# Packed attention and MoE: the narrowing of the first two weight steps placed later in the first attention

## The chip, the cores and the metric

The kernel runs on one core of a Trainium2 chip. Its time is the device time of one execution in microseconds (us). The median of the runs shown is 772.96 us (771.65 to 775.1, 3 runs). One more execution was recorded by the hardware profiler; every row quoted here is from such a record.

Engines go by their names in the profile: PE is the tensor engine's matmuls, PEld its weight loads, DVE the vector engine, ACT the scalar engine, POOL GpSimd, SP the engine whose queue issues the DMAs. Times within the record count from the span's start. L148 is line 148 of the kernel.

## What is computed

```python
q, k, v: (8, 8, 576, 64) float32   # batch, head, token, head dimension; q, k and p drawn 8 times larger
p: (8, 8, 32, 64) float32          # 32 packing vectors for each head
w_in: (512, 2048), w_out: (2048, 512)

def sm_attn(qq, kk, vv):
    s = scale * np.matmul(qq, kk.transpose(0, 1, 3, 2))
    s = s - np.max(s, axis=-1, keepdims=True)
    a = np.exp(s)
    a = a / (np.sum(a, axis=-1, keepdims=True) + 1e-09)
    return np.matmul(a, vv)

p_packed = sm_attn(p, k, v)                # 32 rows for each head
out = sm_attn(q, p_packed, p_packed)
x = out.transpose(0, 2, 1, 3).reshape(8 * 576, 512)
h = x @ w_in
g = h * np.clip(h + 3.0, 0.0, 6.0) / 6.0
return (g @ w_out).astype(np.float32)
```

The two weights reach the kernel as 64-bit floats, so it has to make 32-bit floats of them itself. This is what the text calls narrowing.

## The kernel before, in words

**Tiling.** The eight batches are taken one after another, 576 tokens each. The hidden dimension of 2048 is cut into 16 steps `f` of 128. The product of attention and `w_in` is never made from the attention's output: since the second attention multiplies its weights A (576 x 32 for each head) with the packed rows, the kernel makes M = packed rows x `w_in` once for each batch and then A x M. All large products are made in float32r with each operand split into an upper half (`hi`, a cast) and a lower half (`lo`, what the cast leaves), so a product is three matmuls: hi x hi, hi x lo, lo x hi.

**A weight's way.** `load_w(f)` (L114) loads 128 x 512 64-bit values of `w_in` or `w_out`. `narrowed` (L130) is a generator, advanced one piece at a time by `step(part, n)` and to its end by `rest(part)`:

1. ACT scales the low words (L142), then the high words (L144)
2. DVE shifts the high words (L148), then puts the sign back (L150)
3. POOL adds the low part (L154); the float32 value is done and the load's buffer is free

`w_out_step` (L160) goes on: ACT casts the upper half (`wo_hi`, L164) and DVE makes the lower half (`wo_lo`, L166). For `w_in` the next user is `u_m0` (L192), which makes M of one step: matmuls on PE (L198), a cast on ACT (`m_hi`, L209), the lower half on DVE (`m_lo`, L211). The buffers for the 64-bit values are two for each of `w_in` and `w_out`; steps 2 and 3 use other space (`early`), which batch 0's v and q hold before.

**The first attention** (`first_attention`, L461) makes batch 0's attention, which nothing can hide, and its order is written out by hand for PE, DVE, ACT and POOL, by the sequence of the calls at L706 to L804. Heads come in two groups of four: `b0` and `b1` are `s2(0)` and `s2(1)` (L632), the second scores and their softmax for one group. One `s2` makes, piece by piece: the scores (L641), two maxima (L665), the subtraction (L668) and exponential (L669), the sums (L672), their reciprocals (L674, L676), the normalisation on POOL for group 0 and on DVE for group 1 (L682, L685), two transpositions on PE (L694) with a cast each (`a_hi`, L700), and the lower halves (`a_lo`, L703). Group 1's scores need its packed rows: `pack(1)` makes them (L621, L629), `pt1` turns them (L347) and copies them into place (L351). `tq` and `turned_rest` turn q on PE (L542, L555) and copy it on ACT (L546, L562). `tail()` hands out four banks of PSUM in turn. `warm(n)` (L724) is `n` matmuls on zeros, used by nobody; how many stand where is the tuple `WARM` (L35). `gemm1(h, 0, g)` (L446) is the first product of step 0 for one group.

**The first MoE** (`first_moe`, L899) takes batch 0 through the 16 steps. In each step: the first product (`gemm1`, L453), M of the next step, the narrowing of `w_in` two steps ahead (`in_(f + 2)`), relu on ACT (L956) and the gate on DVE (L957), then the rest of `w_out` of the next step (`rest(out_(f + 1))`) and the first five pieces of `w_out` two steps ahead, the two halves of the gated value (`gh`, L965, on ACT; `gl`, L967, on POOL), and the second product of the step before (`gemm2`, L858). For steps 0 to 3 the order is again written by hand for the four engines, by the sequence of the calls; from step 4 (`IN_ORDER`) on a planner sets it, and batch 1's attention is woven in. SP's order is the planner's throughout. `first_moe` receives the weight generators as `first_attention` leaves them and goes on from where they stand. Batches 1 to 7 follow in `moe`.

Of the kernel before, what the change touches and what calls it, by code (L numbers as in the profile page):

```python
# [31 lines left out]
POOL = range(8, 13)  # L32


WARM = (3, 2, 2, 1, 3)  # L35


@with_exitstack
def packed_attention_moe(
# [90 lines left out]
    def narrowed(f, name):  # L130

        raw = raws.pop((name, f))
        if not wide_in:
            state["w", name, f] = raw
            return
        words = raw.rearrange("p (n two) -> p n two", two=2)  # L140
        low, high = words[:, :, 0], words[:, :, 1]
        nc.scalar.activation(out=low, in_=low.bitcast(U32), func=AF.Copy, scale=2.0 ** -29)  # L142
        yield
        nc.scalar.mul(high.bitcast(F32), high.bitcast(F32), 2.0 ** -112)  # L144
        yield
        x = w_in_at(f) if name == "in" else wp.tile([P, DM], F32, name="x_out")
        xi = x.bitcast(I32)
        nc.vector.tensor_scalar(out=xi, in0=high, scalar1=3, scalar2=None, op0=ALU.logical_shift_left)  # L148
        yield
        nc.vector.scalar_tensor_tensor(  # L150
            out=xi, in0=high, scalar=SIGN, in1=xi, op0=ALU.bitwise_and, op1=ALU.bitwise_or
        )
        yield
        nc.gpsimd.tensor_tensor(out=xi, in0=xi, in1=low, op=ALU.add)  # L154
        state["w", name, f] = x

    def w_in_step(f):
        yield from narrowed(f, "in")

    def w_out_step(f):  # L160
        yield from narrowed(f, "out")
        yield
        x = state.pop(("w", "out", f))
        nc.scalar.copy(out=wo_hi[:, f], in_=x)  # L164
        yield
        (nc.gpsimd if f in POOL else nc.vector).tensor_sub(out=wo_lo[:, f], in0=x, in1=wo_hi[:, f].bitcast(F32))  # L166
# [3 lines left out]
    def step(part, n=1):  # L170
        for _ in range(n):
            next(part, None)

    def rest(*parts):
        for part in parts:
            for _ in part:
                pass
# [268 lines left out]
    def gemm1(h, f, g):  # L446

        mh, ml = state["m", 0, 0]
        fs = slice((f % FPC) * P, (f % FPC + 1) * P)
        ah, al = state["a", 0, g]  # L450
        for hf in range(2):
            for i, (mm, aa) in enumerate(((mh, ah), (mh, al), (ml, ah))):
                nc.tensor.matmul(  # L453
                    h[:, hf, :HS],
                    mm[:, g, fs],
                    aa[:, hf * HS:(hf + 1) * HS],
                    start=(g == 0 and i == 0),
                    stop=(g == NG - 1 and i == 2),
                )

    def first_attention():  # L461


        def tail():
            return ps_o.tile([P, 512], F32, name="ps_t", tag="acc")
# [83 lines left out]
        def turned_rest(nats, copy):  # L549

            t = gp.tile([P, 2, REM], F32, name="qtr0", tag="osb", bufs=2)
            ps = tail()[:, :2 * REM]
            for x, nat in enumerate(nats):
                for h in range(2):
                    nc.tensor.matmul(  # L555
                        ps[64 * h:64 * h + 64, x * REM:(x + 1) * REM],
                        nat[:REM, h, 4],
                        ident[:REM, :REM],
                        start=True,
                        stop=True,  # L560
                    )
            copy(out=t.rearrange("p x r -> p (x r)"), in_=ps)  # L562
            return t
# [160 lines left out]
        def warm(n):  # L724
            ps = tail()
            for _ in range(n):
                nc.tensor.matmul(ps[:, :2 * P], zeros[:, :P], zeros, start=True, stop=True)

        warm(WARM[0])
        act, dve = nc.scalar.copy, nc.vector.tensor_copy  # L730
# [20 lines left out]
        win0, wout0 = w_in_step(0), w_out_step(0)  # L751
# [8 lines left out]
        b0, b1 = s2(0), s2(1)  # L760
        m0, m1 = u_m0(0, tail), u_m0(1, tail)
        win1, wout1 = w_in_step(1), w_out_step(1)
        step(b0)
        rest(win0)
        step(wout0, 3)
        step(win1, 2)
        step(b0, 3)
        pack(1, *et1, r1, v1)
        step(tq[2])
# [1 line left out]
        qt.append(next(tq[2]))  # L771
        step(tq[3])
        qtr.append(turned_rest((q2, q3), act))
        rest(win1)
        rest(pt1)
        qt.append(next(tq[3]))
        step(b0, 4)
        step(wout0, 2)
        step(wout1, 2)
        step(b1)  # L780
        step(b0, 2)
        step(m0, 2)
        step(b1, 3)
        rest(m0)
        rest(b0)
        step(m1, 2)
        step(wout0)
        win2, wout2 = w_in_step(2), w_out_step(2)
        step(win2, 2)
        step(wout2, 2)  # L790
        warm(WARM[1])
        h = ps_h0.tile([P, 2, 512], F32, name="ps_h0", tag="w")
        gemm1(h, 0, 0)
        step(b1, 4)
        warm(WARM[2])
        step(b1, 2)
        warm(WARM[3])
        rest(m1)
        rest(b1)
        rest(wout0)  # L800
        step(wout1, 3)
        gemm1(h, 0, 1)
        warm(WARM[4])
        return h, {2: win2}, {1: wout1, 2: wout2}  # L804

    HAND = {mybir.EngineType.PE, mybir.EngineType.DVE, mybir.EngineType.Activation, mybir.EngineType.Pool}
# [236 lines left out]
```

## Time and profile before

| what | value |
| --- | --- |
| median of the runs shown | 772.96 us |
| the profiled execution: its time | 772.0 us |
| the profiled execution: its span, first to last instruction | 770.2 us |
| mean granted clock of PE | 0.991 |
| PE / DVE / ACT / POOL busy over the span | 741.4 / 374.2 / 388.6 / 288.5 us |
| PE busy in 0 to 40 us, by tens | 7.86, 9.44, 7.71, 8.36 |
| DVE busy in 0 to 40 us, by tens | 1.60, 6.36, 6.23, 8.85 |
| DVE busy in 40 to 100 us, by tens | 8.83, 9.90, 10.00, 9.93, 9.93, 9.81 |

The page gives the engines' busy time over the whole span and in 40 slices, then the chain that ended last. For one stretch, the windows view gives each engine's busy time in it, and the timeline gives the instructions with start, duration, engine, line, operation, output and inputs, and in brackets how long the engine had stood idle and what ended that. "x8" joins eight instructions of one kind. An instruction's duration can hold time in which it waits for a port, and the last 0.07 us or so of one overlap the next on its engine.

### The profile page before, as it was taken

The numbers are of one execution on the slowest core, as the hardware profiler recorded it, in microseconds if no ns is written. First come the engines' busy times: TensorE is split into PE (matmuls) and PEld (weight loads), VectorE is DVE, ScalarE is ACT, GpSimd is POOL, SyncE is SP. The second block draws the span as 40 slices with busy tenths as digits, with TensorE's granted clock in tenths as the row PEclk, the third lists the DMA queues.
The fourth block names the chain that finished last, engine by engine and source line by source line (L and its number), as shares of the span: only waits on it lengthen the run. The fifth ranks groups of instructions, "written<-read, shape, count | busy, mean of one in ns | idle before, by whom it ended". The sixth has DMA issues, their size and how long they took to land.

```text
span 770.2 us, 14036 instructions
## 1 busy us (share of the span) xinstructions
PE 741.4 (96%) x5197; PEld 585.9 (76%) x5197; DVE 374.2 (49%) x741; ACT 388.6 (50%) x922; POOL 288.5 (37%) x420
## 2 busy tenths in 40 slices
PE   8888778999999999999999999999999999999998
PEld 6666566778877786788787886878777887888886
DVE  3799989824283428342553528333452427321111
ACT  4667775455254535563354635454354545453343
POOL 0376795432223323433333332343333233343332
PEclk9999799999999999999999999999999999999999
DMA  8848993213340424015220344005330210000010
GB/s 248 253 108 191 220 244 71 46 55 62 67 103 1 89 66 90 1 46 102 49 65 1 74 82 90 1 29 93 65 73 1 59 33 28 1 29 0 1 42 29
DMA packets 191205, 55.98 MB, mean 73 GB/s; under 512 B 173216, under 2 KB 184480, under 8 KB 191136
## 3 DMA queue, kind: packets, MB, share of 16 engines
q1 hardware_dynamic: 191136, 55.08, 31.1%
q8 instruction: 41, 0.67, 0.4%
q14 instruction: 28, 0.23, 0.1%
HBM read 45.61 MB, written 9.44 MB: 71 GB/s over the span
## 4 chain that ended last, share of the span: by engine, by line
PE 77%; DVE 10%; DMA 5%; issue 3%; SPq 2%; ACT 2%; POOL 1%; DVEq 0%; POOLq 0%; ACTq 0%
PE acc L858 45%; PE ps_hh L829 22%; PE ps L270 6%; DMA raw_in<-in_moe_w_in_dram 2%; DVE tr L403 2%; PE ps L325 1%; DMA nat<-in_k_dram 1%; DVE wo_lo L166 1%; SPq L218 1%; DVE x_out L148 1%; DVE w_in_sb L150 1%; DMA raw_out<-in_moe_w_out_dram 1%; PE ps_h L453 1%; DMA v_nat<-in_v_dram 1%; PE ps L309 1%
## 5 line engine op out<-in xcount | busy, mean ns | idle before, releaser
L847 POOL TENSOR_TENSOR g<-t,g 128x256 fp32r<-128x256 f32 x224 | 167.5, 751 | 411.2 <-ACT g L846 385.1
L858 PE MATMUL acc<-wo_hi,g 128*128 128x512 f32 x896 | 316.7, 395 | 1.5 <-ACT g L846 1.5
L842 DVE SCALAR_TENSOR_TENSOR t<-t,ps_hh 128x320 f32<-128x320 f32 (+1 forms) x224 | 100.1, 449 | 251.8 <-ACT t L841 251.8
L841 ACT ACTIVATE t<-ps_hh,three 128x320 f32<-128x320 f32 (+1 forms) x224 | 112.5, 503 | 178.2 <-PE ps_hh L829 169.9
L858 PEld LDWEIGHTS acc<-wo_hi,g 128*128 128x128 f32 x896 | 167.9, 188 | 36.0 <-issue 4.0
L858 PE MATMUL acc<-wo_lo,g 128*128 128x512 f32 x448 | 177.5, 396 | 0.0
L846 ACT CAST g<-t 128x256 fp32r<-128x256 f32 x224 | 90.3, 405 | 93.1 <-DVE t L842 91.9
L829 PE MATMUL ps_hh<-a_hi,m_hi 128*128 128x320 f32 (+1 forms) x448 | 136.3, 305 | 0.3 <-DVE t L842 0.2
L829 PE MATMUL ps_hh<-a_lo,m_hi 128*128 128x320 f32 (+1 forms) x448 | 132.8, 296 | 0.0
L829 PE MATMUL ps_hh<-a_hi,m_lo 128*128 128x320 f32 (+1 forms) x448 | 132.7, 296 | 0.0
L829 PEld LDWEIGHTS ps_hh<-a_hi,m_hi 128*128 128x128 f32 x448 | 84.4, 189 | 34.5 <-issue 19.9
L858 PEld LDWEIGHTS acc<-wo_lo,g 128*128 128x128 f32 x448 | 84.5, 189 | 11.9 <-issue 1.7
L829 PEld LDWEIGHTS ps_hh<-a_lo,m_hi 128*128 128x128 f32 x448 | 84.5, 189 | 8.1 <-issue 0.9
L829 PEld LDWEIGHTS ps_hh<-a_hi,m_lo 128*128 128x128 f32 x448 | 84.5, 189 | 1.7 <-issue 1.3
L403 DVE STREAM_TRANSPOSE tr<-nat 128x576 f32<-128x576 f32 x56 | 41.7, 764 | 27.7 <-DMA nat<-in_q_dram 11.1
L393 DVE TENSOR_TENSOR m_lo<-ps,m_hi 128x512 fp32r<-128x512 f32 x56 | 36.1, 683 | 35.1 <-ACT m_hi L392 35.1
L853 POOL TENSOR_TENSOR bnd_lo<-t,bnd_hi 128x64 fp32r<-128x64 f32 x112 | 38.6, 344 | 0.0
L392 ACT CAST m_hi<-ps 128x512 fp32r<-128x512 f32 x56 | 30.1, 589 | 10.1 <-PE ps_hh L829 8.2
L270 PE MATMUL ps<-w_in_sb,pps 64*32 64x512 f32 x448 | 34.3, 601 | 0.4 <-DVE m_lo L393 0.4
L453 PE MATMUL ps_h<-a_hi,m_hi 128*128 128x288 f32 x64 | 20.9, 327 | 10.4 <-DVE t L957 9.5
L967 POOL TENSOR_TENSOR gl<-t,gh 128x512 fp32r<-128x512 f32 x16 | 23.1, 1446 | 19.4 <-ACT bnd_hi L966 14.7
L154 POOL TENSOR_TENSOR w_in_sb<-w_in_sb,raw_in 128x512 int32<-128x512 int32 x14 | 19.5, 1395 | 28.5 <-DVE w_in_sb L150 24.5
(175 smaller groups left out, 918.8 us busy)
## 6 DMA issues: line engine op xcount, KB each, us to landing
out_dram<-osb SPq DMA_DIRECT2D x36, 256.0 KB, 2.1
nat<-in_k_dram SPq DMA_DIRECT2D x112, 72.0 KB, 2.6
nat<-in_q_dram SPq DMA_DIRECT2D x112, 72.0 KB, 2.5
raw_in<-in_moe_w_in_dram SPq DMA_DIRECT2D x14, 512.0 KB, 5.0
raw_out<-in_moe_w_out_dram SPq DMA_DIRECT2D x14, 512.0 KB, 4.9
v_nat<-in_v_dram SPq DMA_DIRECT2D x56, 128.0 KB, 3.0
spare<-in_k_dram SPq DMA_DIRECT2D x2, 512.0 KB, 4.9
raw<-in_moe_w_in_dram SPq DMA_DIRECT2D x2, 512.0 KB, 3.9
```

The costliest lines, as they stand in the source:

```text
L270: nc.tensor.matmul(banks[x][NPK * a:NPK * a + NPK, :n], rows[half, a], c, start=True, stop=True)
L392: nc.scalar.copy(out=hi[:, x], in_=ps)
L393: nc.vector.tensor_sub(out=lo[:, x], in0=ps, in1=hi[:, x].bitcast(F32))
L403: nc.vector.transpose(out=t, in_=state.pop(("nat", which, b, a)))
L453: nc.tensor.matmul(h[:, hf, :HS], mm[:, g, fs], aa[:, hf * HS:(hf + 1) * HS], start=(g == 0 and i == 0), stop=(g == NG - 1 and i == 2),)
L829: nc.tensor.matmul(h[:, :n], mm[:, g, fs], aa[:, t0:t0 + n], start=(g == 0 and i == 0), stop=(g == NG - 1 and i == 2),)
L841: nc.scalar.activation(out=t[:, :n], in_=h, func=AF.Relu, bias=three)
L842: nc.vector.scalar_tensor_tensor(out=t[:, :n], in0=t[:, :n], scalar=6.0, in1=h, op0=ALU.min, op1=ALU.mult)
L846: nc.scalar.copy(out=gh, in_=tm)
L847: nc.gpsimd.tensor_sub(out=gl, in0=tm, in1=gh.bitcast(F32))
L853: nc.gpsimd.tensor_sub(out=bnd_lo[:, slot:slot + REM], in0=tb, in1=bh.bitcast(F32))
L858: nc.tensor.matmul(acc, gg, ww[:, f], start=(f == 0 and i == 0), stop=(f == NF - 1 and i == 2),)
```

## The change

Within the first attention, four things move, and nothing is computed otherwise.

- `w_in` of step 1 (`win1`): its scalings go from ahead of group 0's maxima to behind group 1's scores; its DVE and POOL pieces go from ahead of group 1's packed rows to behind group 1's normalisation.
- `w_out` of step 0 (`wout0`): its scalings go from ahead of group 0's maxima to behind group 0's lower halves; its other pieces go behind the first product of step 0, in one go with its two halves.
- M of step 1 (`m1`): from ahead of the first product of step 0 to behind it.
- `w_out` of steps 1 and 2: `wout1` now leaves this function with its scalings issued, where it had its add issued; `wout2` leaves it not begun, where it had its scalings issued. `first_moe`, which isn't edited, goes on from there.

`WARM` has 3, 2, 2 and 2 matmuls in place of 3, 2, 2, 1 and 3.

```diff
-WARM = (3, 2, 2, 1, 3)
+WARM = (3, 2, 2, 2)
...
         step(b0)
         rest(win0)
-        step(wout0, 3)
-        step(win1, 2)
         step(b0, 3)
         pack(1, *et1, r1, v1)
         step(tq[2])
...
         qtr.append(turned_rest((q2, q3), act))
-        rest(win1)
         rest(pt1)
         qt.append(next(tq[3]))
         step(b0, 4)
-        step(wout0, 2)
-        step(wout1, 2)
         step(b1)
+        step(win1, 2)
         step(b0, 2)
         step(m0, 2)
         step(b1, 3)
         rest(m0)
         rest(b0)
-        step(m1, 2)
-        step(wout0)
-        win2, wout2 = w_in_step(2), w_out_step(2)
-        step(win2, 2)
-        step(wout2, 2)
+        step(wout0, 2)
         warm(WARM[1])
         h = ps_h0.tile([P, 2, 512], F32, name="ps_h0", tag="w")
         gemm1(h, 0, 0)
         step(b1, 4)
+        rest(win1)
         warm(WARM[2])
         step(b1, 2)
+        rest(b1)
+        gemm1(h, 0, 1)
+        step(m1, 2)
+        rest(wout0)
+        win2, wout2 = w_in_step(2), w_out_step(2)
+        step(win2, 2)
+        step(wout1, 2)
+        rest(m1)
         warm(WARM[3])
-        rest(m1)
-        rest(b1)
-        rest(wout0)
-        step(wout1, 3)
-        gemm1(h, 0, 1)
-        warm(WARM[4])
         return h, {2: win2}, {1: wout1, 2: wout2}
```

## The prediction, made before the result was known

> **What bounds the kernel now.** The page first.
>
> ```profile
> span 770.2 us, 14036 instructions
> PE 741.4 (96%) x5197; PEld 585.9 (76%) x5197; DVE 374.2 (49%) x741; ACT 388.6 (50%) x922; POOL 288.5 (37%) x420
> PE   8888778999999999999999999999999999999998
> DMA  8848993213340424015220344005330210000010
> ```
>
> A slice is 19.26 us. From the eighth on PE is full; what can be won or lost lies in the first seven, where PE is waiting. The edit lies at 20 to 40 us, so I ask what PE waits for there and just behind, with the busy times by stage.
>
> ```profile
> 36.68:52.54 15.86, 13.22 (x76) 10.09 (x75) 14.55 (x19) 8.93 (x18) 10.99 (x9) 1.00 0.53 116
> 80.00:90.00 10.00, 7.65 (x45) 5.26 (x44) 9.93 (x16) 7.79 (x16) 7.50 (x7) 0.66 0.95 207
> ```
>
> Columns: stretch, length, busy time of PE, PEld, DVE, ACT, POOL, then clock, DMA share, GB/s. DVE is the bound from the last lower half of the attention on (36.68): 14.55 of 15.86 us, and 9.93 of 10 later. But part of that is waiting for POOL. The timeline, DVE, POOL and ACT, around the first steps of the MoE:
>
> ```profile
> 36.68 0.68 DVE L166 TENSOR_TENSOR wo_lo<-x_out,wo_hi 128x512 fp32r<-128x512 f32 x1
> 37.27 0.42 DVE L148 TENSOR_SCALAR x_out<-raw_out 128x512 int32<-128x512 int32 x1
> 37.61 0.42 DVE L148 TENSOR_SCALAR w_in_sb<-raw 128x512 int32<-128x512 int32 x1
> 37.95 0.68 DVE L150 SCALAR_TENSOR_TENSOR x_out<-raw_out,x_out 128x512 int32<-128x512 int32 x1
> 39.15 0.74 DVE L957 SCALAR_TENSOR_TENSOR t<-t,ps_h 128x576 f32<-128x576 f32 x1
> 40.35 1.30 POOL L154 TENSOR_TENSOR w_in_sb<-w_in_sb,raw 128x512 int32<-128x512 int32 x1
> 40.41 0.62 ACT L164 CAST wo_hi<-x_out 128x512 fp32r<-128x512 f32 x1 [1.89 <-POOL x_out L154]
> 40.94 0.62 ACT L965 CAST gh<-t 128x512 fp32r<-128x512 f32 x1
> 41.07 1.13 DVE L166 TENSOR_TENSOR wo_lo<-x_out,wo_hi 128x512 fp32r<-128x512 f32 x1 [1.17 <-ACT wo_hi L164]
> 41.61 0.70 ACT L142 ACTIVATE raw<-raw 128x512 int32<-128x512 uint32 x1
> 41.63 1.71 POOL L967 TENSOR_TENSOR gl<-t,gh 128x512 fp32r<-128x512 f32 x1
> 42.12 1.50 DVE L148 TENSOR_SCALAR x_out<-raw 128x512 int32<-128x512 int32 x1
> 42.20 0.66 ACT L144 ACTIVATE raw<-raw 128x512 f32<-128x512 f32 x1
> 46.33 0.74 DVE L957 SCALAR_TENSOR_TENSOR t<-t,ps_h 128x576 f32<-128x576 f32 x1
> 52.54 0.74 DVE L957 SCALAR_TENSOR_TENSOR t<-t,ps_h 128x576 f32<-128x576 f32 x1
> 58.80 0.74 DVE L957 SCALAR_TENSOR_TENSOR t<-t,ps_h 128x576 f32<-128x576 f32 x1
> ```
>
> Three things. L148 takes 0.42 us alone and 1.50 while POOL's gl runs (until 43.34, and 43.34 + 0.28 is its end); L166 0.68 alone, 1.13 beside POOL's add: one waits for the other, in both directions (gl has 1.71). Each weight costs DVE, POOL, ACT and DVE in a row: L148, L150, the add (1.30), wo_hi (0.62), wo_lo. Where wo_lo is written right behind them, DVE stands still meanwhile (the 1.17). And the orders written by hand hold: only at the seam of the two procedures is one engine's order chosen by what is ready (step 2's L148 at 37.61 ahead of step 1's L150 at 37.95). L957 of steps 0 to 3 stand at 39.15, 46.33, 52.54 and 58.80; they are my clock.
>
> **The front: what the change takes away.**
>
> ```profile
> 20.41 0.22 PE L641 MATMUL ps_w<-pp_bd,qtr 128*64 128x64 f32 x1
> 21.35 0.68 ACT L142 ACTIVATE raw_out<-raw_out 128x512 int32<-128x512 uint32 x1 [2.48 <-DMA raw_out<-in_moe_w_out_dram]
> 21.81 1.09 PE L542 MATMUL ps_t<-ident,spare 128*64 128x128 f32 x16
> 22.64 0.43 DVE L148 TENSOR_SCALAR x_out<-raw_out 128x512 int32<-128x512 int32 x1 [2.58 <-ACT raw_out L144]
> 23.09 0.88 DVE L665 TENSOR_REDUCE mx<-ps_w 128x16 f32<-128x512 f32 x2
> 24.70 0.33 DVE L629 TENSOR_SCALAR pn<-ps_w,rinv 128x128 f32<-128x128 f32 x1
> 25.08 0.33 PE L347 MATMUL ps_t<-ident,pn 128*128 128x128 f32 x1 [2.18 <-DVE pn L629]
> 25.34 1.09 PE L542 MATMUL ps_t<-ident,spare 128*64 128x128 f32 x16
> 29.44 0.88 DVE L665 TENSOR_REDUCE mx<-ps_w 128x16 f32<-128x512 f32 x2 [1.01 <-PE ps_w L641]
> 34.05 0.97 DVE L685 TENSOR_TENSOR z<-z,dn 128x256 f32<-128x256 f32 x2
> 34.94 0.41 DVE L211 TENSOR_TENSOR m_lo<-ps_t,m_hi 128x256 fp32r<-128x256 f32 x1
> 35.57 0.43 DVE L703 TENSOR_TENSOR a_lo<-ps_t,a_hi 128x256 fp32r<-128x256 f32 x1 [0.22 <-ACT a_hi L700]
> 36.27 0.49 DVE L703 TENSOR_TENSOR a_lo<-ps_t,a_hi 128x320 fp32r<-128x320 f32 x1 [0.27 <-ACT a_hi L700]
> 37.78 0.74 ACT L956 ACTIVATE t<-ps_h,three 128x576 f32<-128x576 f32 x1 [1.55 <-PE ps_h L453]
> ```
>
> Now ACT waits 2.48 us for a w_out transfer, L148 on DVE waits for ACT, and group 0's maxima (L665, 23.09) stand behind L148, though their scores are done at 20.63. Without that they start at 20.68: 2.4 earlier. pn follows at 22.28, but PE is then in L542 until 22.90, so L347 comes at 22.94: 2.14 earlier. PE then runs on as now to group 1's scores, whose maxima fall from 29.44 to 27.3. Step 1's M (its product, cast and lower half) leaves this stretch, which frees 0.3 us in front of group 0's lower halves; with the 2.13 of these scores, L685, the normalisation, falls from 34.05 to 31.6. Behind it DVE now has M's lower half (L211) and then waits 0.22 and 0.27 for the casts of the turned weights. In the new order it has the two operations of step 1's w_in there: L148 0.42 and L150 0.68, of which 0.07 overlaps the next, together 1.06. That is 0.6 more than what it takes the place of at the first L703 (35.57 becomes 33.6) and nearly nothing at the second, which waits for its cast: 36.27 becomes 33.95. **Front: -2.3 us.** L956, the relu of step 0, comes 1.0 after the end of the second L703, so it could go at 35.5 in place of 37.78. Bounds: -2.5 if w_in hides fully, -2.0 if the first L703 sets the end.
>
> **Behind it: what the change adds.** I lay the instructions one by one in the new order: each starts when its engine is free and its inputs are there, with the durations above (alone), 0.04 us from one engine to the next (40.41 behind the add's end), 0.13 from DVE to POOL, and DVE and POOL one at a time where both have weights.
>
> Step 0. The end of the second L703 is at 34.4. POOL's add for step 1's w_in runs 33.8 to 35.1. w_out of step 0 comes next: L148 waits for that add and ends at 35.4, L150 at 36.1, add 36.2 to 37.5, wo_hi to 38.2, wo_lo at 38.24, M's lower half to 39.2. On ACT, the two scalings of step 2's w_in stand behind that wo_hi: 38.1 to 39.35. So step 2's L148 and L150 run 39.4 to 40.5 and L957, behind them on DVE, at 40.45 in place of 39.15. The relu was long ready; DVE's order holds it. **+1.3.**
>
> Step 1. w_out of step 1 is now narrowed wholly here. L148 meets the add of w_in 2 (40.65 to 41.95), L150 ends at 42.95, add to 44.4, wo_hi to 45.0, wo_lo at 45.08. On ACT the scalings (L142, L144) of w_out 2, to 46.2, gh, to 46.7, a small cast, and the scalings of w_in 3, to 48.0, queue behind that wo_hi, though their data have long been there. So L148 of w_in 3 is at 48.06 and, with POOL's gl beside it, L957 at 49.45; before it is at 46.33. **+3.1.**
>
> Step 2. Of w_out 2 only L148 has run by then, where the kernel before comes to this point with its add done and has only the cast and wo_lo left. L150 waits for the add of w_in 3 and ends at 51.5, its own add at 52.9, wo_hi at 53.6, wo_lo stands at 53.63. The scalings of w_out 3, gh, and the scalings of w_in 4 follow on ACT (to 56.6), the last pair on DVE, and L957 is at 58.1, before 52.54: 5.6. The same ladder laid for the kernel before gives 39.27, 46.75, 53.15 and 59.55, late by 0.1, 0.4, 0.6 and 0.75, so by differences it is +1.2, +2.7, +5.0 and, for step 3, +5.1. From step 2's end on both kernels issue the same work in the same order, and the third wait is the last.
>
> In brief: the front gives 2.3. Three waits of add and cast (1.30 + 0.13 + 0.62 + 0.08 = 2.1 each) stand on DVE where there was one of 1.17: +5.1. Moved on to DVE's path: w_out 0's pair 0.94, M's half 0.34, and 0.75 for POOL's add: +2.0. Together +4.8; the ladder's 5.0 is what I take. Bounds: +2.7 (the third wait falls beside work), +7 (gl, which falls 6.7 behind in the ladder, sets the step instead of L957).
>
> The Trainium skill ("SBUF — State Buffer", Who interferes with whom) says that a DVE instruction with two SBUF inputs, or in a two-port mode, is blocked for the whole of a GpSimd instruction that holds the shared ports. Taken at its worst, all four moved instructions (L148 and L150 of two weights) meet a whole add, 5.2 in place of my 0.75, and the sum would be +9.4; the 1.50 above shows the block, but DVE and POOL mostly take turns here.
>
> Other moved things cost nothing. Four warming matmuls at the end become two, and two fewer stand in all: PE waits there anyway. The queue of SP is passed as well:
>
> ```profile
> 26.23 1.28 POOL L154 TENSOR_TENSOR w_in_sb<-w_in_sb,raw_in 128x512 int32<-128x512 int32 x1 [4.70 <-DVE w_in_sb L150]
> 27.87 1.57 SPq L127 DMA_DIRECT2D raw_in<-in_moe_w_in_dram  x2
> 59.46 0.30 DVE L246 STREAM_TRANSPOSE p_tr<-p_nat 128x128 f32<-128x128 f32 x1
> ```
>
> The second of these two loads needs the buffer of step 1's w_in, which the add on POOL frees: at 35.1 in place of 27.5. If SP stands there, batch 1's p and k come up to 7.3 us later, with their first use at 59.46: hidden. The loads into the buffers that the last q leaves go 2 us sooner, and nobody waits for them. Bound: 0 to 1.
>
> Does the delay last? DVE stays full to 90 (the row above), PE's slices are full only from about 135, and nothing of PE's work is removed, so it is handed on: 772.0 for the profiled execution (span 770.2 and 1.8 around it) becomes 777.0. The median of the runs shown is 772.96, one above that execution; on it, **778.0**.
>
> **Rivals.**
> First, the gain stays: the seam's rule (what is ready goes first) holds more widely than I think, L957 of step 0 goes at 36.2 and other work fills the three waits. Price -2.3: 770.6, to 768 if later waits shrink too. Against it: rows of steps 0 to 3 keep the written order. It decides if step 0's L957 is ahead of step 2's L148. Chance 0.18.
> Second, the delay is swallowed: the DMA line has its 9s from 77 to 116, and if transfers set that stretch, 5 us at its start are made up. Price 0: 773. Against it: the loads there wait for buffers that DVE and POOL free. Chance 0.17.
> Third, PE's clock falls in the new gaps and PE becomes the bound of the next two steps. PE stands for 4.5 us (36.7 to 41.2) in the ladder. Its share of a step is 13.22 of 15.86, some 5.2 us of 6.2; at the 0.66 of the row of 80:90 that is 7.8, 1.6 over the step, 3.2 for two: 5.0 + 3.2 = 8.2, 780.2 on the profiled execution, 781 on the median. Against it: in that very row DVE still has 9.93 of 10 and sets the step. The Trainium skill ("TensorE: Matmul & The Clock Gate", HAM oscillation) has PE at half clock after some 3.4 us of idling: by that rule step 1's products would slow here, into room that ACT's order leaves: by the ladder relu 1 can't go before 47.9, and the products end at 43. Chance 0.10.
>
> **How the numbers follow.** My case has 0.55, from 775.7 (+2.7) to 780 (+7). About 0.5%, 3.9 us, can be told from no change here, so slower begins at 776.8: 0.42 of my case and the third rival, 0.52. Faster is half of the first rival, 0.09. The rest, 0.39, is within. The range leaves out the better half of the first rival and what lies above the third: 770.6 to 781.5. My case alone: 775.7 to 780.
>
> **What would show it.** Right: group 0's maxima at about 20.7, group 1's at 27.3, the relu of step 0 near 35.5, but L957 of steps 0 to 3 near 40.4, 49, 57.6 and 64, with three DVE waits of about 2 us ended by wo_hi in front of L166. Wrong: L957 of step 0 before 38, or of step 3 before 60; or the same delay at step 3 and none at 140 us (the second rival).

## The result, and the profile after

The changed kernel has a median of 783.83 us (781.04 to 787.5, 6 runs), the kernel before 773.0 (771.6 to 775.88, 6 runs on the same chip). The ratio is 1.0138, with a 95% interval of 1.01 to 1.0175: slower by 10.7 us, between 7.7 and 13.5. The profiled execution took 786.55 us with a span of 784.6, 14.4 above that of before; it is the second longest of the six, so its record holds more loss than the 10.7 us of the medians. The forecast was 778.0; the direction was right, the size less than half.

The page of the changed kernel (the same four lines as of before, with PE's clock):

```profile
span 784.6 us, 14026 instructions
PE 745.4 (95%) x5193; PEld 589.9 (75%) x5193; DVE 364.0 (46%) x741; ACT 388.1 (49%) x922; POOL 288.0 (37%) x420
...
PE   7779677999999999999999999999999999999998
...
PEclk9969888999999999999999999999999999999999
DMA  8827894310542054105240154105240120000010
```

As before, PE is full from the eighth slice (of 19.6 us) on: what was lost was lost ahead of 137 us or so. PE's clock stands at 0.6 in the third slice and at 0.8 in the fifth to seventh; the kernel before has one dip, 0.7 in the fifth:

```profile
PEclk9999799999999999999999999999999999999999
```

So there are two places to look at, and the gates of the steps tell them apart. The timeline of the changed kernel, DVE and ACT; lines from 804 on stand five earlier than before, so that L952 is the gate that was L957, L951 the relu:

```profile
19.59 0.88 DVE L665 TENSOR_REDUCE mx<-ps_w 128x16 f32<-128x512 f32 x2 [0.18 <-PE ps_w L641]
26.10 0.88 DVE L665 TENSOR_REDUCE mx<-ps_w 128x16 f32<-128x512 f32 x2 [2.11 <-PE ps_w L641]
34.23 0.74 ACT L951 ACTIVATE t<-ps_h,three 128x576 f32<-128x576 f32 x1 [1.73 <-PE ps_h L453]
36.89 0.69 DVE L166 TENSOR_TENSOR wo_lo<-x_out,wo_hi 128x512 fp32r<-128x512 f32 x1 [2.09 <-ACT wo_hi L164]
38.02 0.43 DVE L148 TENSOR_SCALAR w_in_sb<-raw 128x512 int32<-128x512 int32 x1
39.09 0.75 DVE L952 SCALAR_TENSOR_TENSOR t<-t,ps_h 128x576 f32<-128x576 f32 x1
43.71 0.69 DVE L166 TENSOR_TENSOR wo_lo<-x_out,wo_hi 128x512 fp32r<-128x512 f32 x1 [2.11 <-ACT wo_hi L164]
47.87 0.75 DVE L952 SCALAR_TENSOR_TENSOR t<-t,ps_h 128x576 f32<-128x576 f32 x1
52.06 0.69 DVE L166 TENSOR_TENSOR wo_lo<-x_out,wo_hi 128x512 fp32r<-128x512 f32 x1 [2.12 <-ACT wo_hi L164]
56.40 0.74 DVE L952 SCALAR_TENSOR_TENSOR t<-t,ps_h 128x576 f32<-128x576 f32 x1
62.72 0.74 DVE L952 SCALAR_TENSOR_TENSOR t<-t,ps_h 128x576 f32<-128x576 f32 x1
104.49 0.76 DVE L952 SCALAR_TENSOR_TENSOR t<-t,ps_h 128x576 f32<-128x576 f32 x1 [0.93 <-ACT t L951]
131.16 0.74 DVE L952 SCALAR_TENSOR_TENSOR t<-t,ps_h 128x576 f32<-128x576 f32 x1
164.47 0.76 DVE L952 SCALAR_TENSOR_TENSOR t<-t,ps_h 128x576 f32<-128x576 f32 x1 [3.43 <-ACT t L951]
```

Up to step 3 it went as the ladder had it: group 0's maxima early, relu 0 at 34.23, and then the three waits of 2.1 us each on wo_hi. The gate of step 3 is 3.9 us behind (62.72 against 58.80), that of step 6 still 3.7 (85.17 against 81.52). The rest comes later: step 7 is 7.4 behind (104.49 against 97.06), step 10 12.1 (131.16 against 119.10), step 15 14.9 (164.47 against 149.60). That is the part which the forecast did not have.

What differs there? In the timelines of both kernels the orders of the engines agree from step 4 to step 6, but not behind. The planner's orders from step 4 on are written out as lists in two of the kernels below (f_after and f_before). Compared place by place, 45 of DVE's 160 entries differ, 51 of ACT's 180, 174 of PE's 700, 12 of POOL's 70 and none of SP's 200. In the timeline of the kernel before, the differences begin at 95 us, behind step 6, and lie mostly ahead of step 15; behind some 167 us the orders are the same again. So the recorded sentence "from step 2's end on both kernels issue the same work in the same order" is false. But the clock and the DMA rows changed in that stretch too, so it is not yet shown to be the cause.

Three theories, then. **A**: the ladder's delay is handed on 1:1, and the rest is the price of the other order. **B**: the waits open gaps on PE, its clock falls, and the slower products lengthen the later steps (the third rival, larger). **C**: the weights, later by 4 us, meet the full DMA stretch of 77 to 116 us.

### The profile page after: what moved, and what is told of

Read it like the earlier page. It is cut to its first block, busy times and chain, and to the rows that moved or that the text cites. A ratio compares the mean times of both kernels' runs of the same rounds, so it can differ in the third digit from the quotient of the medians.

```text
span 784.6 us, 14026 instructions
## 1 busy us (share of the span) xinstructions
PE 745.4 (95%) x5193; PEld 589.9 (75%) x5193; DVE 364.0 (46%) x741; ACT 388.1 (49%) x922; POOL 288.0 (37%) x420
## 4 chain that ended last, share of the span: by engine, by line
PE 77%; DVE 6%; DMA 5%; ACT 3%; SPq 2%; issue 2%; POOL 1%; DVEq 0%; ACTq 0%; POOLq 0%
PE acc L853 45%; PE ps_hh L824 22%; PE ps L270 6%; DMA raw_in<-in_moe_w_in_dram 2%; DMA nat<-in_k_dram 2%; PE ps_h L453 1%; PE ps L325 1%; SPq L218 1%; DVE tr L403 1%; PE ps L309 1%; POOL x_out L154 1%; SPq L256 1%; DVE wo_lo L166 1%; DVE w_in_sb L150 1%; DMA raw_out<-in_moe_w_out_dram 1%
## 5 line engine op out<-in xcount | busy, mean ns | idle before, releaser
L403 DVE STREAM_TRANSPOSE tr<-nat 128x576 f32<-128x576 f32 x56 | 41.8, 766 | 31.8 <-PE ps L270 12.8
L453 PE MATMUL ps_h<-a_hi,m_hi 128*128 128x288 f32 x64 | 23.2, 362 | 14.2 <-DVE t L952 11.3
L962 POOL TENSOR_TENSOR gl<-t,gh 128x512 fp32r<-128x512 f32 x16 | 23.1, 1443 | 36.4 <-ACT gh L960 24.1
L270 PE MATMUL ps<-w_in_sb,pps 64*32 64x512 f32 x448 | 34.3, 601 | 0.5 <-DVE m_lo L393 0.5
L853 PE MATMUL acc<-wo_hi,gh 128*128 128x512 f32 x64 | 28.3, 442 | 6.7 <-ACT gh L960 6.7
```

What stands on the lines that cost most here:

```text
L270: nc.tensor.matmul(banks[x][NPK * a:NPK * a + NPK, :n], rows[half, a], c, start=True, stop=True)
L403: nc.vector.transpose(out=t, in_=state.pop(("nat", which, b, a)))
L453: nc.tensor.matmul(h[:, hf, :HS], mm[:, g, fs], aa[:, hf * HS:(hf + 1) * HS], start=(g == 0 and i == 0), stop=(g == NG - 1 and i == 2),)
L853: nc.tensor.matmul(acc, gg, ww[:, f], start=(f == 0 and i == 0), stop=(f == NF - 1 and i == 2),)
```

## The experiments

A table of the gates first, in us from the span's start, from the DVE rows of each profiled execution; the last column is step 15 less step 0.

| kernel | step 0 | step 3 | step 6 | step 10 | step 15 | 15 less 0 |
| --- | --- | --- | --- | --- | --- | --- |
| before | 39.15 | 58.80 | 81.52 | 119.10 | 149.60 | 110.45 |
| changed | 39.09 | 62.72 | 85.17 | 131.16 | 164.47 | 125.38 |
| again | 38.70 | 62.36 | 84.63 | 128.43 | 161.23 | 122.53 |
| io_before | 42.57 | 62.19 | 95.17 | 124.48 | 172.28 | 129.71 |
| io_after | 41.29 | 64.70 | 97.70 | 129.93 | 177.67 | 136.38 |
| e_nowait | 37.24 | 59.37 | 80.97 | 124.59 | 156.82 | 119.58 |
| f_after | 40.98 | 64.43 | 85.71 | 124.92 | 155.35 | 114.37 |
| f_before | 38.45 | 58.04 | 80.76 | 123.26 | 156.20 | 117.75 |
| f_nowait | 37.80 | 60.00 | 82.69 | 121.54 | 151.98 | 114.18 |
| f_onewait | 41.43 | 62.12 | 84.80 | 124.70 | 155.35 | 113.92 |
| e_m1 | 42.09 | 61.71 | 84.41 | 122.40 | 152.96 | 110.87 |
| f_pps | 37.59 | 57.25 | 78.61 | 117.59 | 152.31 | 114.72 |
| f_g1 | 38.39 | 54.92 | 76.47 | 116.54 | 146.96 | 108.57 |
| f_g5 | 40.22 | 56.14 | 78.63 | 117.47 | 147.88 | 107.66 |

Step 0 varies by a few us between executions, since the loads of the front start a little earlier or later and for a reason told in the last section; so spacings are compared, and the times by their ratios. A spacing from step 0 leaves out what happens ahead of it, so it compares only kernels with the same pieces there: f_nowait has nearly f_after's last column, but its step 0 stands 3.2 us earlier and its time is 4.7 us shorter.

**again: the changed kernel once more.** No edit.

> The changed kernel, unchanged, once more, for a second record of it. Six runs of it spread over 781 to 787.5 us, and the longer ones have the lower clock. Theory A: the gates of steps 0 to 16 stand within 1 us of the first record's, whatever the clock. Theory B: where the clock of this run is higher than 0.976, the time is shorter by some 0.8 us for each 0.001, and the steps in which the first record shows products at half clock are the shorter ones here.

783.51 us, clock 0.978. Up to step 6 the gates are within 0.6 us of the first record's, as A has it; step 15 is 3.2 us earlier, which A did not have. So the stretch from step 7 on is not only slow in the changed kernel, it varies as well. The longer execution has the lower clock, but it is 3 us longer and not the 1.6 that B's rate gives.

**io_before and io_after: both kernels with the order written by hand through all 16 steps.**

```diff
-IN_ORDER = 4
+IN_ORDER = 99
```

> The kernel before, with the order written by hand kept through all sixteen steps of the first MoE, so that no planner sets an order that could differ from its partner's. It is the base of its partner and no test by itself: its time may lie some us to either side of the kernel before. All theories: the gate (L957) of steps 0 to 3 stands as in the kernel before, near 39.2, 46.3, 52.5 and 58.8 us.

> The change on top of that base: from step 2's end on, both now really issue the same work in the same order. Theory A (the three added waits of DVE are worth the 4 to 5 us of the ladder, and the rest of the 10.8 us comes from the planner, which orders step 7 and the following otherwise in the changed kernel): slower than its partner by 4 to 6 us, the difference of the gates standing at +4 from step 3 on. Theory B (PE's granted clock falls in the new gaps and the slower products lengthen the steps behind) and theory C (the later weights meet the stretch in which the DMA engines are full): the difference grows behind step 6 all the same, and it is slower by 9 to 12 us; under B with PE's clock in the stretches of 80 to 160 us lower than its partner's, under C with more waiting for raw_in.

797.82 us (794.61 to 799.48) and 800.02 (798.89 to 802.7). The spacing from step 0 to step 3 is 3.8 us larger with the change (23.41 against 19.62), and at step 9 it is 3.8 still (78.79 against 74.96): the delay is handed on in full so far. At step 10 it grows to 6.7, and then lies between 6.2 and 7.4, though the orders of DVE, ACT, PE and POOL are the same in both from step 4 to the end. Ahead of io_after's gate of step 10 DVE waits for a load of q, for which io_before does not wait:

```profile
128.20 0.78 DVE L403 STREAM_TRANSPOSE tr<-nat 128x576 f32<-128x576 f32 x1 [3.05 <-DMA nat<-in_q_dram]
```

So the same order hands a delay on 1:1 only until a transfer comes too late. The medians differ by 2.2 only, less than any theory had. In the profiled execution of io_before the front ran at a low clock, so that its step 0 stands at 42.57 in place of 39. A base 24 us slower than the kernel before is no good base, and the pair settles nothing about the rest.

**f_after and f_before: the two orders exchanged.** The order that the planner chose for one kernel, from step 4 on, is written into the other, as edges of issue order between consecutive instructions of each engine:

```diff
+ORDER = {
+    'DVE': [(63, 2), (69, 1), (33, 2), (39, 1), (44, 1), (37, 1), (45, 1),
...
+}
...
             if f == IN_ORDER:
+                begin.append(len(nc.cur_bb.bb.instructions))
                 hand.close()
...
+    traced = nc.cur_bb.bb.instructions
+    for runs in ORDER.values():
+        at = [begin[0] + i + j for i, n in runs for j in range(n)]
+        for a, b in zip(at, at[1:]):
+            tc.add_manual_dep(traced[b], traced[a].name, ...
```

> The changed kernel, up to step 3 unchanged, from step 4 on with each engine issuing its instructions in exactly the order that the planner chose for the kernel before. Theory A (the ladder's delay is handed on 1:1 and the rest comes from the planner's other order from step 7 on): the gates stand 3.5 to 6 us behind the kernel before all the way to step 15, and the time is 776.5 to 779. Theory B (PE's clock in the gaps) and theory C (weights arriving in the full DMA stretch): both act whatever the order, so the gates fall 9 us or more behind by step 10 and the time is 782 or more.

> The kernel before, up to step 3 unchanged, from step 4 on with each engine issuing its instructions in exactly the order that the planner chose for the changed kernel. Theory A: slower than the kernel before by 4 to 7 us though nothing of the change itself is in it (777 to 780), the gates standing even with the kernel before up to step 6 and falling behind from step 7 on, mostly between steps 9 and 11. Theories B and C: no more than 1.5 us slower (773 to 774.5), since neither the gaps nor the later loads are there.

f_after, the change with the old order: 778.21 us (776.92 to 779.38, 12 runs), ratio 1.0046 (1.0027 to 1.0065): 3.6 us slower, between 2.1 and 5.0. f_before, the old front with the other order: 778.7 us (774.85 to 782.5, 11 runs), ratio 1.0059 (1.0033 to 1.0085): 4.6 us slower, between 2.6 and 6.6. Rows of f_after, where the gate is L962, and the last gate of the kernel before:

```profile
40.98 0.75 DVE L962 SCALAR_TENSOR_TENSOR t<-t,ps_h 128x576 f32<-128x576 f32 x1
64.43 0.74 DVE L962 SCALAR_TENSOR_TENSOR t<-t,ps_h 128x576 f32<-128x576 f32 x1
155.35 0.75 DVE L962 SCALAR_TENSOR_TENSOR t<-t,ps_h 128x576 f32<-128x576 f32 x1 [0.18 <-ACT t L961]
```

```profile
149.60 0.76 DVE L957 SCALAR_TENSOR_TENSOR t<-t,ps_h 128x576 f32<-128x576 f32 x1 [0.15 <-ACT t L956]
```

Step 0 to step 3 takes 23.45 us against 19.65, 3.8 more; step 0 to step 10 takes 83.94 against 79.95, 4.0 more, and to step 15 114.37 against 110.45, 3.9 more. In between it swings (2.4 at step 6, 4.6 at step 7), but with the same order the delay of step 3 comes out at the end to 0.1 us, clock and full DMA stretch included. That is A, and against B and C for this order. f_before, which has nothing of the change, is even with the kernel before from step 0 to step 6 (42.31 against 42.37) and loses 7.3 us from there to step 15. The two prices sum to 8.2 us; the whole was 10.7, and its interval of 7.7 to 13.5 holds the sum. By the spacings of the table they sum to 11.2 us (3.9 and 7.3), against 14.9 in the changed kernel's first record and 12.1 in its second.

What the sum may lack is a sign of theory C in the changed kernel's own record. From the gate of step 4 to that of step 15, ACT waits 12.8 us in all for loads of w_in there, and 9.1 in the second record; it is 3.2 in the kernel before, 3.5 in f_after and 0.9 in f_before. The longest:

```profile
87.43 0.65 ACT L142 ACTIVATE raw_in<-raw_in 128x512 int32<-128x512 uint32 x1 [3.81 <-DMA raw_in<-in_moe_w_in_dram]
```

So C is out with the old order behind the change, but not where the other order and the later loads come together. No run separates that.

Where does the other order lose it? Step 10 of the kernel before, DVE and PE:

```profile
119.10 0.74 DVE L957 SCALAR_TENSOR_TENSOR t<-t,ps_h 128x576 f32<-128x576 f32 x1
120.10 0.27 DVE L342 COPY pps<-ps 128x128 f32<-128x128 f32 x1
120.91 1.77 DVE L166 TENSOR_TENSOR wo_lo<-x_out,wo_hi 128x512 fp32r<-128x512 f32 x1
121.75 0.71 PE L270 MATMUL ps<-tr,pps 64*32 64x288 f32 x16
123.34 0.68 DVE L166 TENSOR_TENSOR wo_lo<-x_out,wo_hi 128x512 fp32r<-128x512 f32 x1
```

and the same step of f_before, whose lines stand nine or ten later (L175 is L166, L351 is L342, L967 the gate, L279 is L270), with one row of its chain view at the end:

```profile
120.76 0.68 DVE L175 TENSOR_TENSOR wo_lo<-x_out,wo_hi 128x512 fp32r<-128x512 f32 x1
121.70 1.44 DVE L175 TENSOR_TENSOR wo_lo<-x_out,wo_hi 128x512 fp32r<-128x512 f32 x1
123.06 0.28 DVE L351 COPY pps<-ps 128x128 f32<-128x128 f32 x1
123.26 0.74 DVE L967 SCALAR_TENSOR_TENSOR t<-t,ps_h 128x576 f32<-128x576 f32 x1
123.39 1.22 PE L279 MATMUL ps<-tr,pps 64*32 64x288 f32 x16 [3.15 <-DVE pps L351]
...
124.61 3.18 PE ps_h L462 x12
```

Before, the gate and then a copy of 0.27 us for batch 1's attention (pps) go first, the narrowing behind them. In the other order both stand behind two lower halves of w_out. PE waits 3.15 us for that copy, and the twelve matmuls of the next first product then take 3.18 us in one piece, where the kernel before has:

```profile
119.99 1.84 PE ps_h L453 x12
```

So the clock does fall and cost, as B says, but in gaps that the other order opens, and in a kernel without the change.

**f_pps: one place of that order alone.** The kernel before in its own order, with only the copy moved on DVE, in step 10:

```diff
 L148 w_in, L166, L150 w_in, L166 of step 10
-L342 pps   (ahead of these four)
+L342 pps   (behind them)
```

> The kernel before in its own planned order, but for one instruction of 0.27 us: in step 10 the copy of the turned packed rows for batch 1 (pps, L342) stands on DVE behind that step's w_in pair and the two lower halves (L148, L166, L150, L166) instead of ahead of them, where the order that the planner chose for the changed kernel has it. PE's next matmuls (L270) read it, and the second product stands behind them in PE's order. If the other order costs by such single places (a copy that PE waits for, put behind narrowing), PE stands still for some 2.5 us (from 121.7 to 124.3), its clock may halve for the products behind, and the time is 1 to 3 us above the kernel before. If it costs by the narrowing as a whole, coming earlier or later, this one place costs nothing that can be told: within 0.8 us.

776.11 us (775.03 to 781.84, 12 runs), ratio 1.0035 (1.0009 to 1.0062): 2.7 us slower, between 0.7 and 4.8. That is the first of the two outcomes above, though the interval reaches down to the second's 0.8. Rows of DVE and PE:

```profile
122.43 0.28 DVE L351 COPY pps<-ps 128x128 f32<-128x128 f32 x1
122.76 0.87 PE L279 MATMUL ps<-tr,pps 64*32 64x288 f32 x16 [2.44 <-DVE pps L351]
...
124.16 0.63 PE L867 MATMUL acc<-wo_lo,gh 128*128 128x512 f32 x1
124.58 0.63 PE L867 MATMUL acc<-wo_hi,gh 128*128 128x512 f32 x1
```

PE stands for 2.44 us, and the matmuls of the second product behind it take 0.63 us each, where they take 0.40 elsewhere in the same record. Steps 0 to 10 take what they take before (80.00 against 79.95), steps 10 to 12 4.1 us more. The copy stands 4.84 us behind the step's gate instead of 1.00. By the medians, this one instruction of 0.27 us, put 3.8 us later, costs over half of what the whole other order costs; the two intervals (0.7 to 4.8, 2.6 to 6.6) leave the share open. Within f_before the place weighs less: of its 7.3 us, 1.4 are lost from step 6 to 9, 2.3 from step 9 to 12 and 3.6 from step 12 to 15, where no place was tried alone.

**e_nowait and f_nowait: the change without two of its three waits.** The last pieces of the changed front in another order, so that w_out of steps 1 and 2 leaves the first attention as in the kernel before (add issued, scalings issued). This takes back the fourth of the four moves; the other three stay. It was run once with the planner's own order behind (e_nowait), once with the order of the kernel before (f_nowait):

```diff
-        gemm1(h, 0, 1)
-        step(m1, 2)
-        rest(wout0)
         win2, wout2 = w_in_step(2), w_out_step(2)
         step(win2, 2)
         step(wout1, 2)
+        step(wout2, 2)
+        gemm1(h, 0, 1)
+        step(m1, 2)
+        step(wout0, 3)
         rest(m1)
+        step(wout1, 3)
+        rest(wout0)
```

> The changed kernel with its last pieces put in another order, so that each lower half (L166) on DVE has other DVE work between it and the add and the cast it waits for: by the same ladder the gates of steps 0 to 3 come about 3.7 us earlier than in the changed kernel. Theory A: the waits are what costs, so the gate of step 3 falls from 62.7 to 59 or 60 and the time lies between 774 and 777 us, if the planner's order does not differ again. Theory B: as A if the gaps of PE go with the waits, with a clock of 0.985 or more. Theory C: the loads are issued earlier by the same amount, so it does not tell C from A; a time above 780 with the gates at 59 to 60 would speak against the waits being the cause at all.

> The version of the change without the three waits (L166 always behind other DVE work), from step 4 on in the order that the planner chose for the kernel before. Its first record had the gates of steps 1 to 3 only 0.6 us behind the kernel before, and lost its 6 us behind step 6. Theory A: 773 to 775, within 0.3% of the kernel before. Theories B and C: B 776 or more with a clock under 0.988, C as its first record, 777 to 780.

e_nowait: 779.36 us (779.1 to 782.72, 5 runs), ratio 1.0086 (1.0054 to 1.0117). Its gate of step 3 is where it should be (59.37) and step 6 is even earlier than before (80.97), but the planner chose a third order, step 7 came at 102.37, and the time lies 2.4 us above what A had, whose condition (no other order again) was not met. f_nowait: 773.54 us (772.48 to 774.71, 12 runs), ratio 0.999 (0.9971 to 1.0008), as A had it. Its lower halves, two of the four lines of f_nowait around step 0 and 1:

```profile
40.19 0.69 DVE L175 TENSOR_TENSOR wo_lo<-x_out,wo_hi 128x512 fp32r<-128x512 f32 x1
42.70 0.69 DVE L175 TENSOR_TENSOR wo_lo<-x_out,wo_hi 128x512 fp32r<-128x512 f32 x1 [1.82 <-ACT wo_hi L173]
```

One wait of 1.82 is left, where the kernel before has one of 1.17. With the other two waits gone, and the order the same, the change costs nothing that can be told: f_after less f_nowait, both run together, is 4.7 us, the price of the fourth move, with the waits and what comes late behind them.

**f_onewait: one such wait added to the kernel before.** In the order of the kernel before from step 4 on:

```diff
         step(win2, 2)
-        step(wout2, 2)
```

> The kernel before with one edit, and the planner's order of the kernel before from step 4 on: the two scalings of step 2's w_out are not issued in the first attention, so that they come in step 0 and the cast behind them stands later on ACT. It puts one added wait into step 1 and takes nothing away. Theory A: by the ladder step 1 gains 1.1 us (its M and its narrowing find ACT free sooner), step 2 loses 1.2 and step 3 stands 1.3 us later; handed on, that is 1.3 us on the time, 774 to 776 where the kernel before has 773 to 774. Theory B (a wait costs only what PE's clock makes of it): within 0.5 us of the kernel before, or over 3 us slower, with a clock below 0.988.

775.72 us (772.87 to 780.27, 12 runs), ratio 1.0023 (0.9998 to 1.0047): between no change and 3.6 us, with 1.8 in the middle. The trace has the wait in step 1:

```profile
51.47 0.69 DVE L175 TENSOR_TENSOR wo_lo<-x_out,wo_hi 128x512 fp32r<-128x512 f32 x1 [2.06 <-ACT wo_hi L173]
```

From step 0 to step 3 the spacing is 20.69 us against 19.62 in e_m1, whose front ran at the same clock: 1.1, where the ladder had 1.3. By the time alone it is inconclusive.

**e_m1: M of step 1 behind the first product, alone.**

```diff
-        step(m1, 2)
...
-        rest(m1)
...
         gemm1(h, 0, 1)
+        step(m1, 2)
+        rest(m1)
```

> The kernel before with only one part of the change: M of step 1 is made behind the first product of step 0 in place of ahead of it. The planner's order from step 4 on is that of the kernel before. Theory A: M's lower half (0.34 of DVE's path) only changes places with work that waited for a cast; by the ladder the gate of step 3 moves by -0.2 us, and the time by nothing that can be told: 772.5 to 774.5. A rival (M is late for step 1's product and opens the gap of PE): slower by 2 us or more.

773.46 us (772.23 to 775.76, 10 runs), ratio 0.9985 (0.9964 to 1.0007): nothing that can be told. By that interval this part of the change costs some 0.5 us at most.

**f_g1 and f_g5: the gain of the front kept, the waits avoided.** The sequence of f_g1 from group 0's scores to the end, with w_out's and w_in's pieces handed out singly, against the kernel before, several calls on one line (f_g5 hands out the same pieces at other places); behind it the order of the kernel before:

```diff
         step(b0)
         rest(win0)
-        step(wout0, 3)
-        step(win1, 2)
-        step(b0, 3)
+        step(b0); step(wout0); step(b0); step(wout0); step(b0)
         pack(1, *et1, r1, v1)
+        step(wout1)
         step(tq[2])
+        step(win1)
...
         step(tq[3])
+        step(wout0); step(win1)
         qtr.append(turned_rest((q2, q3), act))
-        rest(win1)
+        step(wout0)
         rest(pt1)
+        step(wout0)
         qt.append(next(tq[3]))
+        step(wout1)
         step(b0, 4)
-        step(wout0, 2)
-        step(wout1, 2)
+        step(win1); step(wout0)
         step(b1)
+        step(win1)
         step(b0, 2)
...
```

> A new order for the first attention and the seam, with the planner's order of the kernel before from step 4 on. It keeps what the change gains in the front (nothing of a weight stands ahead of group 0's maxima on DVE) but puts the pieces of w_out 0, w_in 1 and w_out 1 into the places at 23 to 34 us where DVE stands idle, one by one, so that no lower half stands right behind its add and cast and less of them is left for steps 0 to 2. Theory A (DVE's path through steps 0 to 3 sets the time and is handed on 1:1): by the ladder the gate of step 0 comes 2.8 us earlier than in the kernel before, those of steps 1 to 3 some 6 us earlier; half of that, 3 us, is the least I expect, so 767 to 771. Theory C (the transfers of the later weights set the pace): the gates of steps 0 to 3 come earlier, step 5 or 6 doesn't, and the time is 772 or more.

> A second order of the same kind, with the scalings of w_out 0 and w_in 1 back ahead of group 0's exponential on ACT, and the planner's order of the kernel before from step 4 on. Theory A: by the ladder the gate of step 0 comes 1.5 us earlier, those of steps 1 to 3 some 5 to 6 us earlier, and the time is 767 to 771, within 1 us of the first order's. Theory C: 772 or more.

f_g1: 769.66 us (767.77 to 773.34, 9 runs), ratio 0.9939 (0.9916 to 0.9962), 4.7 us faster than the kernel before. f_g5: 770.76 us (769.45 to 773.28, 12 runs), ratio 0.9956 (0.9935 to 0.9976). Both are faster than both kernels. The gates of f_g1 (L984 here) at steps 0, 3 and 15:

```profile
38.39 0.76 DVE L984 SCALAR_TENSOR_TENSOR t<-t,ps_h 128x576 f32<-128x576 f32 x1 [0.40 <-ACT t L983]
54.92 0.74 DVE L984 SCALAR_TENSOR_TENSOR t<-t,ps_h 128x576 f32<-128x576 f32 x1
146.96 0.75 DVE L984 SCALAR_TENSOR_TENSOR t<-t,ps_h 128x576 f32<-128x576 f32 x1 [0.17 <-ACT t L983]
```

Step 0 came 0.8 us earlier than before and not 2.8, step 3 3.9 earlier and not 6, step 15 2.6 earlier. The times were as A had them and C is out for the second time; the sizes of the steps were not: f_g5's step 0 is 1.1 later than before, where 1.5 earlier was expected, and the two times are 1.1 us apart, not within 1. The gates are single records, and step 0 alone moves by more than 1 us between them.

## Why the prediction was right in direction and wrong in size

**The front, -2.3: right.** The relu of step 0 came 3.55 us earlier (34.23 against 37.78). Not all of that is the edit's: ahead of it, L150 of step 0's w_in already stands at 18.72 in place of 19.36, and the maxima, due at 20.68 by the working, are 1.1 early. That leaves 2.4 to 2.9.

**The three waits and the ladder, +5.0: right.** The waits were forecast at 2.1 each and are 2.09, 2.11 and 2.12. Step by step the ladder has 9.0, 8.65 and 6.5 us from step 0 to step 3; measured are 8.78, 8.53 and 6.32. The gate of step 3 is 3.9 behind in the record, and 4.5 to 5.0 with the earlier start added. That the waits are what costs follows from f_nowait, which has two of them less; since it gets there by taking back the fourth move, the waits are not apart from that move, and f_onewait, which adds one to the kernel before, is inconclusive by its time.

**M of step 1, the warming matmuls, SP's queue at nothing: right** for M by e_m1; the other two were not tried alone, but f_nowait has the change's warming matmuls and its later load of w_in and is even with the kernel before.

**Handed on 1:1: right, for one order.** f_after shows it up to step 15, io_before and io_after up to step 9 (3.8 us at step 3 and at step 9), where a load breaks it. The forecast of 778.0 and f_after's 778.21 agree so closely by luck: the kernel before had 774.14 in that session, not the 772.96 that the forecast starts from. The sum gave +5.0; against its own partner f_after costs 3.6 us, between 2.1 and 5.0.

**The step that failed: "from step 2's end on both kernels issue the same work in the same order".** It holds to step 6. The prediction put the work behind step 2 at nothing beyond the delay handed on. But from step 6 on the planner chose another order for the changed kernel, and that order costs 4.6 us by itself (f_before, between 2.6 and 6.6). In the place that was tried alone, PE is left waiting for a small copy behind narrowing, and its clock halves for what follows.

**The rivals.** The first (the gain stays) is out: step 0's gate (39.09) stood behind step 2's L148 (38.02). The second (swallowed by the transfers) is out by f_after, whose delay is all there at step 15. The third had PE's clock fall in the gap of step 0, and it did. PE's rows of the changed kernel:

```profile
39.98 0.58 PE L453 MATMUL ps_h<-a_hi,m_hi 128*128 128x288 f32 x1 [4.20 <-DVE t L952]
40.36 0.44 PE L453 MATMUL ps_h<-a_lo,m_hi 128*128 128x288 f32 x1
```

A matmul of 0.29 to 0.30 takes 0.44 there. But step 1 was not longer than the ladder for it, and f_after has the same low clock in steps 1 and 2 and loses nothing for it behind them: in the changed kernel the products of step 1 end at 43.2, and relu 1 goes at 46.48. As to the rule of the Trainium skill ("SBUF — State Buffer", Who interferes with whom), taken at its worst, by which the sum would have been +9.4: up to step 3 the change lost 4.5 to 5.0 us, not that.

**What stays open**: which of the other places of the second order cost what step 10 doesn't, above all from step 12 to 15; how much of the 2.5 us between the sum of the two prices and the whole the later loads make; and why the changed kernel's two records differ by 3 us, of which ACT's waits for w_in (12.8 and 9.1) are a sign and not yet the cause.

## What to carry to other kernels

Where a scheduler orders the work behind an edit, an edit changes that order too: list the order of both kernels to the end before saying "the same from here on", and measure the edit with the old order pinned behind it. f_nowait, f_g1 and f_g5 kept or bettered the time of the kernel before with its order pinned. A hand-over chain of several engines (shift, add, cast, lower half) cost some 2.1 us of DVE's time here wherever the last link stood right behind the others in DVE's order, and none in f_nowait's row of 40.19, where other work stands between. And look at what PE waits for in small copies of other work: a gap of a few us on PE can be paid twice, once as the wait and once as the slow matmuls behind it.

## What the runs showed of the hardware

A gap on PE need not be long to halve its clock, and its length alone does not decide. The kernel before has one in the front, ahead of L347. In its record it is 2.18 us (the row of 25.08 above) and the clock stays at 1.00; group 1's scores behind it:

```profile
26.75 1.10 PE L641 MATMUL ps_w<-pp_bd,qt 128*128 128x64 f32 x8
```

In e_m1, whose front has the same instructions up to there, it is 2.49:

```profile
24.81 0.33 PE L347 MATMUL ps_t<-ident,pn 128*128 128x128 f32 x1 [2.49 <-DVE pn L629]
...
27.03 1.97 PE L641 MATMUL ps_w<-pp_bd,qt 128*128 128x64 f32 x8
```

The same eight matmuls take 1.97 in place of 1.10. In all fourteen records the granted clock changes only after 3.41 us or a whole multiple of it. So each record can be cut into windows of 3.41 us by the moments of these changes. Here are the windows around the gap, first of e_m1, then of the kernel before; the first number behind the length is PE's busy time, the third from the end the granted clock:

```profile
22.28:25.69 3.41, 0.92 (x15) 0.76 (x15) 3.26 (x8) 2.56 (x6) 0.00 (x0) 1.00 0.83 284
25.70:35.94 10.24, 10.24 (x56) 8.18 (x51) 5.39 (x16) 4.46 (x11) 4.34 (x6) 0.50 0.78 228
```

```profile
20.89:24.30 3.41, 2.01 (x31) 1.43 (x27) 1.63 (x4) 2.45 (x4) 0.64 (x2) 1.00 0.52 165
24.30:27.72 3.42, 2.64 (x33) 2.27 (x33) 3.27 (x11) 2.16 (x6) 1.28 (x1) 1.00 0.62 236
```

In e_m1 the whole gap lies in one window, PE is busy for 0.92 of 3.41 us, and half clock follows for three windows. In the kernel before an edge at 24.30 cuts the gap in two, and PE is still busy for 2.01 and 2.64 us of the two windows. The same shows where two gaps have the same length, ahead of the same matmul behind step 6's gate, in the kernel before and in f_before:

```profile
82.97 0.79 PE L858 MATMUL acc<-wo_hi,gh 128*128 128x512 f32 x1 [2.31 <-ACT gh L965]
```

```profile
82.21 0.51 PE L867 MATMUL acc<-wo_hi,gh 128*128 128x512 f32 x1 [2.31 <-ACT gh L975]
```

The first lies mostly in one window (PE busy for 1.74 of 3.41 us) and half clock follows at 82.33; the second is cut by an edge at 81.37 (1.94 and 2.58) and the clock stays. Counted over the fourteen records up to 170 us: of the windows at full clock, all 52 in which PE was busy for less than 46% were followed by half clock, none of the 458 with more than 60%, and 7 of the 31 between. So a gap of 2.11 us was enough in f_nowait (41.12 to 43.24), and one of 2.31 was not in f_before.

Of the six records with the front of the kernel before, three lost the clock behind this gap (io_before, f_onewait, e_m1) and three did not (before, f_before, f_pps). From that L347 to step 0's gate it is 17.3 to 17.5 us in the first three and 14.07 in each of the others. In the records of the changed front the clock is 1.00 from 25 to 30 us, since that gap is gone. So the change also removes something that costs the kernel before some 3.3 us in a part of its executions. The times of before may hold both kinds, which would make the prices above look smaller than the spacings of the gates do; no run shows that by itself.

The Trainium skill ("TensorE: Matmul & The Clock Gate", HAM oscillation) warns of PE gaps above some 3.4 us. Here 2.11 (f_nowait), 2.44 (f_pps) and 2.49 (e_m1) were enough; where the two differ, the measurement decides. The same page (Part 1: The HAM clock gate) says that the window in which the activity is counted runs freely, so that the moment varies. The traces agree: the edges stand at other moments in each record, 24.30 in the kernel before and 25.70 in e_m1, and a gap costs by how it falls between them.
